# A gated-MLP kernel behind attention: six batches' output projection by seven block products

## The chip, the cores and the metric

The kernel runs on one core of a Trainium2 chip. The metric is the device time of one execution in microseconds. TensorE (PE) does the matmuls and writes their results into eight PSUM banks; VectorE (DVE), ScalarE (ACT) and GpSimd (POOL) work on what lies in the banks or in SBUF (POOL here on SBUF alone); SyncE (SP) issues most of the transfers. Each engine works through its own list in order, and waits where an operand isn't there or a buffer isn't free.

## The reference

Attention with 16 query heads on 4 key and value heads, then a gated MLP with a spatial unit, for 8 batches of 384 tokens. Cut to what matters:

```python
x = attention(q, k, v)                       # (8, 384, 1024)
h = np.maximum(x @ w_in, 0.0)                # w_in (1024, 1024)
u, v = h[..., :512], h[..., 512:]
v_n = (v - mean(v)) / np.sqrt(var(v) + 1e-06)
v_s = np.einsum('ts,bsd->btd', w_spatial, v_n) + b_spatial[None, :, None]
gated = u * v_s                              # (8, 384, 512)
return gated @ w_out                         # w_out (512, 1024)
```

The last line, 384 x 512 by 512 x 1024 for each batch, is what the change is about.

## The kernel before

Tokens come in three tiles of 128 per batch (`NT`), so there are 6 sets of attention work per batch (`SETS`: three tiles by two halves of the heads) and 18 units (`UNITS`). The scores of a set fill six PSUM banks (`units`, L267), ACT takes their exponentials (`exp`, L291), and `weigh` (L295) multiplies them with v, two groups a set, of twelve narrow matmuls each, whose results DVE normalizes by a reciprocal and a product (L315, L317) into `x16`. A transposing transfer (`x_send`, L338) makes `xt` of it.

Everything behind attention is a generator, `gated` (L514), which runs about half a batch behind attention: `pour` (L727) takes matmuls from it in portions of planned time between the parts of a set, so that TensorE's list is a mix of both. For each batch it yields

- `v_part` (L350), three times eight matmuls of 512 columns, into a bank that DVE empties (`vr`, L371); DVE then takes the statistics (`bn_stats`, `bn_aggr`, L383 and L384);
- `u_part` (L433), four blocks of eight matmuls of 384 columns, emptied by ACT (L449). While these run, `root` and `norm` (L386, L393) make the factors on ACT and DVE (`nmr`, L396) and POOL makes `vn` (L401);
- `s_part` (L452), four times three matmuls of 384 columns, to which DVE adds the bias (`vs`, L469) and which POOL multiplies with u into `gT` (L474; DVE does a third of the very last one, L477);
- `o_part` (L482), the output projection: for each of the three token tiles two halves of 512 columns, four matmuls each (L496), copied from the bank into `osb` by DVE, or by ACT for the second half of tile 1 (and others in the last batch), and sent out by SP when both halves are there (L511).

The projection of batch b is made in the generator's batch b + 1: two half tiles behind its first `v_part`, then one ahead of each `s_part` and one behind the last (L517 to L551). In batch 7 one stands behind v and five around s. Batch 7's own projection ends the kernel.

Which bank a group gets is decided when the kernel is written out: `bank` (L79) takes the one that a small model of the engines holds to be free first. `spend` adds planned TensorE time, and `reads` adds the time that an engine is expected to take to empty the bank. Work on DVE that isn't told to the model by a `reads` doesn't exist for it. On the chip TensorE then waits for the real release. `at` (L594) hangs other work, such as casts and loads, on a unit's number.

Of the kernel before, what the change touches and what calls it, by code (L numbers as in the profile page):

```python
# [9 lines left out]
FP32 = mybir.dt.float32  # L10
FP16 = mybir.dt.float16
I32 = mybir.dt.int32
AF = mybir.ActivationFunctionType
ALU = mybir.AluOpType
# [4 lines left out]
def kernel(  # L19
# [14 lines left out]
    nc = tc.nc  # L34
# [52 lines left out]
    def spend(ns):  # L87
        clock[nc.tensor] += ns
# [234 lines left out]
        measure()  # L323

    def new_xt(b):
        xts[b] = att.tile([P, NK, S], FP16, name=f"xt_{b}", tag="xt", bufs=3)

    def x_turn(b, qt, lo, hi, eng):
        if qt == 0 and lo == 0:
# [20 lines left out]
    def v_part(b, st, lo=0, hi=NK):  # L350
        if st == 0 and lo == 0:
            mvs[b] = small.tile([P, NT, 2], FP32, name=f"mv_{b}", tag="mv")
        if lo == 0:
            pvs[b, st] = bank([P, 512], FP32, f"pv_{b}_{st}")
        pv = pvs[b, st]
        for kt in range(lo, hi):
            nc.tensor.matmul(  # L357
                pv,
                xts[b][:, kt, st * P : (st + 1) * P],
                w_in16[:, kt, DH:DFF],  # L360
                start=(kt == 0),
                stop=(kt == NK - 1),
            )
            spend(C512)
            if kt < NK - 1:
                yield C512
        if hi < NK:
            return
        reads(dve, 610.0, f"pv_{b}_{st}")
        vr = moe.tile([P, DH], FP32, name=f"vr_{b}_{st}", tag="vr", bufs=6)  # L370
        dve.tensor_scalar(vr, pv, 0.0, None, op0=ALU.max)  # L371
        v_r[b, st] = vr
        unmeasured.append((b, st))
        if b == B - 1:
            measure()
        yield C512
# [16 lines left out]
    def norm(b):  # L393
        rstd = mvs[b, "rstd"]
        nmr = small.tile([P, NT], FP32, name=f"nmr_{b}", tag="nmr")
        dve.scalar_tensor_tensor(  # L396
            nmr, mvs[b][:, :, 0], -1.0, rstd, op0=ALU.mult, op1=ALU.mult
        )
        for st in range(NT):
            vn = moe.tile([P, DH], FP16, name=f"vn_{b}_{st}", tag="vn", bufs=6)  # L400
            (dve if b == 0 and st == 1 else pool).tensor_scalar(  # L401
                vn,
                v_r.pop((b, st)),
                rstd[:, st : st + 1],
                nmr[:, st : st + 1],
                op0=ALU.mult,
                op1=ALU.add,
            )
            v_n[b, st] = vn
# [6 lines left out]
    def judge():  # L416


        for i, op in enumerate((ALU.max, ALU.min, ALU.add)):
            dve.tensor_reduce(ext[:, i : i + 1], r_all, axis=mybir.AxisListType.X, op=op)  # L420
        pool.memset(ones16, 1.0)
        pool.tensor_scalar(ext[:, 1:2], ext[:, 1:2], 0.0, None, op0=ALU.is_gt)
        pool.tensor_scalar(ext[:, 0:1], ext[:, 0:1], 1.0, ext[:, 1:2], op0=ALU.is_le, op1=ALU.mult)
        pool.tensor_scalar(fine16, ext[:, 2:3], 0.0, ext[:, 0:1], op0=ALU.is_gt, op1=ALU.mult)
# [52 lines left out]
                eng.tensor_tensor(gT[:, :, t], vs[:, :, t], uT[:, :, t], ALU.mult)  # L477
        yield C384

    osbs = {}  # L480

    def o_part(b, tt, half):  # L482
        last = b == B - 1
        if half == 0:
            osbs[b, tt] = ops.tile([P, DM], FP32, name=f"osb_{b}_{tt}", tag="osb")
        osb = osbs[b, tt]
        rows = out[b].rearrange("(p t) d -> p t d", t=NT)

        on_act = half and (last or tt == 1) or last and tt == NT - 1
        parts = [(half * 512, 512, act if on_act else dve, sp)]  # L490
        if last and tt == NT - 1 and half:
            parts = [(512, 256, dve, sp), (768, 128, act, act), (896, 128, dve, sp)]
        for c0, width, eng, queue in parts:
            po = bank([P, 512], FP32, f"po_{b}_{tt}_{c0}")
            for m in range(NM):
                nc.tensor.matmul(  # L496
                    po[:, 0:width],
                    gTs[b][:, m, tt * P : (tt + 1) * P],
                    w_out16[:, m, c0 : c0 + width],
                    start=(m == 0),  # L500
                    stop=(m == NM - 1),
                )
                spend(C512 * width / 512)
                if m < NM - 1:
                    yield C512 * width / 512
            cols = slice(c0, c0 + width)
            copy(eng, osb[:, cols], po[:, 0:width], f"po_{b}_{tt}_{c0}")
            if last or (b, tt) == (B - 2, NT - 1):
                queue.dma_start(rows[:, tt, cols], osb[:, cols])
            elif half:  # L510
                sp.dma_start(rows[:, tt, :], osb)  # L511
            yield C512 * width / 512

    def gated():  # L514
        for b in range(B):
            u0 = b * UNITS
            behind = [(b - 1, tt, half) for tt in range(NT) for half in range(2)] if b else []  # L517
            if b == 0:
                for st in range(NT):
                    yield ("from", 6 * st + 7)  # L520
                    yield from v_part(b, st, 0, 4)
                    yield ("from", 6 * st + 10)
                    yield from v_part(b, st, 4, 8)
            else:
                yield ("from", u0 + 12)
                yield from v_part(b, 0)
                for _ in range(1 if b == B - 1 else 2):
                    yield from o_part(*behind.pop(0))
                yield ("from", u0 + 18)
                yield from v_part(b, 1)  # L530
                yield ("from", u0 + 24)
                yield from v_part(b, 2)
            for m in range(NM):
                i = 0
                for x in u_part(b, m):
                    yield x
                    i += 1
                    if (m, i) == (1, 6):
                        root(b)
                    if (m, i) == (2, 3):  # L540
                        norm(b)
                    if (b, m, i) == (B - 1, 2, 5):
                        judge()
            for m in range(NM):
                if (b, m) == (B - 1, 2):
                    count()
                if behind:
                    yield from o_part(*behind.pop(0))
                yield from s_part(b, m)
            if behind:  # L550
                yield from o_part(*behind.pop(0))  # L551
        for tt in range(NT):
            for half in range(2):
                yield from o_part(B - 1, tt, half)
# [39 lines left out]
    def at(n, f, *args):  # L594
        todo.setdefault(n, []).append((f, args))
# [92 lines left out]
    at(29, load_v, 2)  # L688
    at(31, load_q, 2, 1, sp, (1, 2))
    at(36, cast_v, 2, pool)  # L690
    for j, n in ((0, 34), (1, 36)):
        at(n, cast_q, 2, j, pool, (1, 2))
        at(n + 1, q_send, 2, j, 1, NT)
# [346 lines left out]
```

## Time and profile before

| what | value |
|---|---|
| runs | 237.82, 238.12, 238.57 us; median 238.12 us |
| profiled execution | 238.65 us, of which its span 237.1 us |
| PE, ACT, DVE, POOL busy | 230.4, 170.0, 143.8, 102.2 us |
| 512-column projection matmuls (L496) | 188, 49.6 us busy, 379 ns each with their overlap |
| copies of `osb` by DVE, 512 wide | 37, 686 ns each |
| copies of `osb` by ACT, 512 wide | 10, 592 ns each |
| `x` (L317), 256 wide; `vs` (L469), 384 wide | 424 and 552 ns each |
| `bn_stats`; `vr` | 685 and 682 ns each |
| f16 evictions `qT` (512 wide), `kT` (384 wide) | 422 and 354 ns each |
| `gT` on POOL (L474); `vn` on POOL (L401) | 1058 and 779 ns each |

Matmul records overlap each other, since a matmul starts before the one ahead has left the pipeline; their pace is the distance of two starts, not the duration of one. An idle time in brackets behind a line of the timeline is that of the engine just before the operation, with what ended it.

### The profile page before, as it was taken

The numbers are of one execution on the slowest core, as the hardware profiler recorded it, in microseconds if no ns is written. First come the engines' busy times: TensorE is split into PE (matmuls) and PEld (weight loads), VectorE is DVE, ScalarE is ACT, GpSimd is POOL, SyncE is SP. The second block draws the span as 40 slices with busy tenths as digits, with TensorE's granted clock in tenths as the row PEclk, the third lists the DMA queues.
The fourth block names the chain that finished last, engine by engine and source line by source line (L and its number), as shares of the span: only waits on it lengthen the run. The fifth ranks groups of instructions, "written<-read, shape, count | busy, mean of one in ns | idle before, by whom it ended". The sixth has DMA issues, their size and how long they took to land.

```text
span 237.1 us, 5954 instructions
## 1 busy us (share of the span) xinstructions
PE 230.4 (97%) x2317; PEld 124.3 (52%) x2317; DVE 143.8 (61%) x382; ACT 170.0 (72%) x350; POOL 102.2 (43%) x149
## 2 busy tenths in 40 slices
PE   7899999999999999999999999999999999999993
PEld 6555655545554545555464555554465455545542
DVE  2668774676447674566646576376744667367561
ACT  2899989959897869977797776986697776401212
POOL 3489493642556442275045800575032500460740
PEclk9999999999999999999999999999999999999999
DMA  6999959999999999699988899479912543240266
GB/s 186 289 300 308 275 152 160 169 317 260 296 211 237 258 351 171 214 199 309 188 257 214 241 214 294 68 271 158 255 27 44 114 164 79 48 177 0 86 229 222
DMA packets 67757, 47.48 MB, mean 200 GB/s; under 512 B 48368, under 2 KB 60576, under 8 KB 67728
## 3 DMA queue, kind: packets, MB, share of 16 engines
q1 hardware_dynamic: 62800, 39.86, 68.9%
q0 software_dynamic: 3952, 6.42, 12.3%
q10 hardware_dynamic: 976, 0.82, 1.1%
q8 instruction: 18, 0.29, 0.5%
q14 instruction: 11, 0.09, 0.1%
HBM read 25.95 MB, written 12.58 MB: 163 GB/s over the span
## 4 chain that ended last, share of the span: by engine, by line
PE 91%; DMA 4%; DVE 2%; issue 0%; ACTq 0%; ACT 0%
PE pu L438 18%; PE pv L357 17%; PE po L496 17%; PE sc L281 15%; PE av L301 14%; PE psp L457 7%; DMA q<-in_q_dram 2%; DMA qT<-q 2%; PE qps L240 1%; PE xps L334 1%; DVE x L317 1%; DVE qT L218 0%; DVE osb L218 0%; DVE q L208 0%; ACTq L124 0%
## 5 line engine op out<-in xcount | busy, mean ns | idle before, releaser
L293 ACT ACTIVATE aT<-sc 128x512 f16<-128x512 f32 x288 | 147.5, 617 | 31.4 <-PE sc L281 30.8
L301 PEld LDWEIGHTS <-aT 128*128 128x128 f16 x1152 | 47.0, 97 | 17.3 <-issue 2.3
L357 PE MATMUL pv<-w_in,xt 128*128 128x512 f16 x192 | 51.0, 380 | 0.1
L301 PE MATMUL av<-v,aT 128*128 128x65 f16 x1152 | 50.5, 193 | 0.1
L496 PE MATMUL po<-w_out,gT 128*128 128x512 f16 (+2 forms) x200 | 50.5, 371 | 0.0
L438 PE MATMUL pu<-xt,w_in 128*128 128x384 f16 x256 | 49.9, 327 | 0.0
L401 POOL TENSOR_SCALAR vn<-vr,rstd,nmr 128x512 f16<-128x512 f32 x23 | 17.6, 779 | 67.0 <-DVE nmr L396 45.6
L474 POOL TENSOR_TENSOR gT<-vs,uT 128x384 f16<-128x384 f32 x31 | 32.4, 1058 | 31.8 <-DVE r_all L315 16.9
L317 DVE TENSOR_TENSOR x<-av,r_all 128x256 f16<-128x256 f32 x96 | 40.7, 424 | 3.3
L281 PE MATMUL sc<-qT,kT 64*128 64x512 f16 x288 | 41.5, 380 | 0.3
L315 DVE RECIPROCAL r_all<-av 128x4 f32<-128x4 f32 x96 | 17.1, 178 | 40.6 <-PE av L301 40.3
L218 DVE COPY osb<-po 128x512 f32<-128x512 f32 (+2 forms) x39 | 26.1, 669 | 16.3 <-PE po L496 16.3
L438 PEld LDWEIGHTS <-w_in 128*128 128x128 f16 x256 | 22.1, 98 | 17.1 <-issue 5.5
L449 ACT ACTIVATE uT<-pu 128x384 f16<-128x384 f32 x32 | 15.8, 495 | 16.0 <-PE pu L438 15.8
L496 PEld LDWEIGHTS <-gT 128*128 128x128 f16 x200 | 17.6, 98 | 17.1 <-issue 3.3
L357 PEld LDWEIGHTS <-xt 128*128 128x128 f16 x192 | 15.8, 97 | 17.8 <-issue 5.5
L281 PEld LDWEIGHTS <-kT 64*128 64x128 f16 x288 | 10.9, 94 | 23.5 <-issue 11.9
L457 PE MATMUL psp<-wsT,vn 128*128 128x384 f16 x96 | 22.2, 327 | 0.0
L469 DVE TENSOR_TENSOR vs<-psp,bias_bc 128x384 f32<-128x384 f32 x32 | 17.6, 552 | 7.1 <-PE psp L457 6.9
L371 DVE TENSOR_SCALAR vr<-pv 128x512 f32<-128x512 f32 x24 | 16.4, 682 | 8.4 <-PE pv L357 8.3
L203 POOL CAST q<-q 128x768 f16<-128x768 f32 x22 | 17.6, 830 | 7.9 <-issue 4.3
L383 DVE BATCH_NORM_STATS2 stats<-vr 128x6 f32<-128x512 f32 x24 | 16.4, 685 | 0.1
(55 smaller groups left out, 103.2 us busy)
## 6 DMA issues: line engine op xcount, KB each, us to landing
out_dram<-osb SPq DMA_DIRECT2D x20, 512.0 KB, 3.9
q<-in_q_dram SPq DMA_DIRECT2D x10, 768.0 KB, 5.7
v_None<-in_v_dram SPq DMA_DIRECT2D x6, 384.0 KB, 7.0
w_in<-in_moe_w_in_dram POOLq DMA_DIRECT2D x4, 512.0 KB, 9.8
k_None<-in_k_dram SPq DMA_DIRECT2D x5, 384.0 KB, 3.8
out_dram<-osb SPq DMA_DIRECT2D x7, 256.0 KB, 2.5
q<-in_q_dram POOLq DMA_DIRECT2D x2, 768.0 KB, 7.6
w_out<-in_moe_w_out_dram POOLq DMA_DIRECT2D x2, 512.0 KB, 9.5
```

The costliest lines, as they stand in the source:

```text
L203: eng.tensor_copy(t16[:, :, :, hh, :], src[:, hh])
L218: (act.copy if eng is act else dve.tensor_copy)(o, i)
L281: nc.tensor.matmul(sc, kTs[b][rows, j, kt * P : (kt + 1) * P], qTs[b, j][rows, qt].rearrange("p (r i c) -> p i r c", r=G, i=G), start=True ...
L293: act.activation(a, sc, AF.Exp, scale=scale)
L301: nc.tensor.matmul(av[:, i * (D + 1) : (i + 1) * (D + 1)], aT[:, kt, hh, i * P : (i + 1) * P], v1[b % 2][:, 2 * j + hh, kt, 0 : D + 1], st ...
L317: dve.tensor_tensor(x16s[b][:, qt, c : c + 256].rearrange("p (i d) -> p i d", i=G), o[:, :, 0:D], r.to_broadcast([P, G, D]), ALU.mult,)
L357: nc.tensor.matmul(pv, xts[b][:, kt, st * P : (st + 1) * P], w_in16[:, kt, DH:DFF], start=(kt == 0), stop=(kt == NK - 1),)
L401: (dve if b == 0 and st == 1 else pool).tensor_scalar(vn, v_r.pop((b, st)), rstd[:, st : st + 1], nmr[:, st : st + 1], op0=ALU.mult, op1=A ...
L438: nc.tensor.matmul(pu[:, 0:S], w_in16[:, kt, m * P : (m + 1) * P], xts[b][:, kt, :], start=(kt == 0), stop=(kt == NK - 1),)
L457: nc.tensor.matmul(psp[:, 0:S], v_n[b, st][:, m * P : (m + 1) * P], wsT16[:, st, :], start=(st == 0), stop=(st == NT - 1),)
L474: pool.tensor_tensor(gT, vs, uT, ALU.mult)
L496: nc.tensor.matmul(po[:, 0:width], gTs[b][:, m, tt * P : (tt + 1) * P], w_out16[:, m, c0 : c0 + width], start=(m == 0), stop=(m == NM - 1),)
```

## The change

For batches 1 to 6 (`fast`), the projection of token tiles 0 and 1 is made as one product of a 2 x 2 block matrix (two token tiles by two halves of the 512 gated features) with a 2 x 2 block matrix (two halves of the features by two halves of the 1024 columns). Seven block products replace the eight; each is two matmuls of 512 columns into a bank of its own (`f_part`). Products 5, 6, 7 and 4 take combined weights, products 5, 6, 7 and 3 combined gated values:

- `w_combine` makes the four combinations of the weights, once, in f16 on DVE, at units 42, 45, 48 and 51 (each 1024 elements a partition);
- `g_combine` makes the four combinations of a batch's gated values in f16 on DVE (256 elements a partition each), in the next batch behind its last `v_part`;
- all sums of products are DVE operations that read a bank: product 1 is copied into `partial`, 6 and 7 are added on top of it and of each other, 2 and 1 give tile 0's first half, 5 is read twice, 4 gives the rest of tile 1 and 3 the rest of tile 0. Tile 1 is sent out behind product 4 and tile 0 behind product 3.

The order within the next batch changes too. Tile 2 is made as before, but right behind the first `v_part`; products 1 and 2 stand behind u's block 0, 6 and 7 behind block 1, 5 behind block 2, 4 ahead of the second `s_part` and 3 ahead of the third. In batch 7, tile 2 of batch 6 stands ahead of the fourth `s_part`, and nothing stands behind that; both of its halves are copied by ACT, where DVE copied them before. Batch 0 and batch 7 keep the eight products. Some buffers become fewer: `xt` two instead of three, `vr` four instead of six, `vn` three instead of six.

```diff
@@ -323,7 +323,7 @@
         measure()
 
     def new_xt(b):
-        xts[b] = att.tile([P, NK, S], FP16, name=f"xt_{b}", tag="xt", bufs=3)
+        xts[b] = att.tile([P, NK, S], FP16, name=f"xt_{b}", tag="xt", bufs=2)
 
     def x_turn(b, qt, lo, hi, eng):
         if qt == 0 and lo == 0:
@@ -367,7 +367,7 @@
         if hi < NK:
             return
         reads(dve, 610.0, f"pv_{b}_{st}")
-        vr = moe.tile([P, DH], FP32, name=f"vr_{b}_{st}", tag="vr", bufs=6)
+        vr = moe.tile([P, DH], FP32, name=f"vr_{b}_{st}", tag="vr", bufs=4)
         dve.tensor_scalar(vr, pv, 0.0, None, op0=ALU.max)
         v_r[b, st] = vr
         unmeasured.append((b, st))
@@ -397,7 +397,7 @@
             nmr, mvs[b][:, :, 0], -1.0, rstd, op0=ALU.mult, op1=ALU.mult
         )
         for st in range(NT):
-            vn = moe.tile([P, DH], FP16, name=f"vn_{b}_{st}", tag="vn", bufs=6)
+            vn = moe.tile([P, DH], FP16, name=f"vn_{b}_{st}", tag="vn", bufs=3)
             (dve if b == 0 and st == 1 else pool).tensor_scalar(
                 vn,
                 v_r.pop((b, st)),
@@ -477,7 +477,78 @@
                 eng.tensor_tensor(gT[:, :, t], vs[:, :, t], uT[:, :, t], ALU.mult)
         yield C384
 
-    osbs = {}
+    osbs, halves16, partial = {}, {}, {}
+    w_out_t = cst.tile([P, 4, 2, 512], FP16, name="w_out_t")
+
+    def fast(b):
+
+        return 0 < b < B - 1
+
+    def w_combine(i):
+
+        b11, b12, b21, b22 = (w_out16[:, r : r + 2, c : c + 512] for r in (0, 2) for c in (0, 512))
+        t = [w_out_t[:, k] for k in range(4)]
+        x, y = ((b12, b11), (b22, t[0]), (b22, b12), (t[1], b21))[i]
+        dve.tensor_tensor(t[i], x, y, ALU.subtract)
+
+    def g_combine(b):
+
+        t = halves16[b] = moe.tile([P, 4, 2, P], FP16, name=f"gS_{b}", tag="gS", bufs=1)
+        a11, a12, a21, a22 = (
+            gTs[b][:, r : r + 2, c : c + P] for c in (0, P) for r in (0, 2)
+        )
+        dve.tensor_tensor(t[:, 0], a21, a22, ALU.add)
+        dve.tensor_tensor(t[:, 1], t[:, 0], a11, ALU.subtract)
+        dve.tensor_tensor(t[:, 2], a11, a21, ALU.subtract)
+        dve.tensor_tensor(t[:, 3], a12, t[:, 1], ALU.subtract)
+
+    def f_part(b, n):
+
+        if n == 2:
+            for tt in range(2):
+                osbs[b, tt] = ops.tile([P, DM], FP32, name=f"osb_{b}_{tt}", tag="osb")
+        if n == 1:
+            partial[b] = moe.tile([P, 3, 512], FP32, name=f"part_{b}", tag="part", bufs=1)
+        g, s, w, t = gTs[b], halves16.get(b), w_out16, w_out_t
+        left, right = {
+            1: (lambda m: g[:, m, 0:P], lambda m: w[:, m, 0:512]),
+            2: (lambda m: g[:, 2 + m, 0:P], lambda m: w[:, 2 + m, 0:512]),
+            3: (lambda m: s[:, 3, m], lambda m: w[:, 2 + m, 512:1024]),
+            4: (lambda m: g[:, 2 + m, P : 2 * P], lambda m: t[:, 3, m]),
+            5: (lambda m: s[:, 0, m], lambda m: t[:, 0, m]),
+            6: (lambda m: s[:, 1, m], lambda m: t[:, 1, m]),
+            7: (lambda m: s[:, 2, m], lambda m: t[:, 2, m]),
+        }[n]
+        name = f"pf_{b}_{n}"
+        po = bank([P, 512], FP32, name)
+        for m in range(2):
+            nc.tensor.matmul(po, left(m), right(m), start=(m == 0), stop=(m == 1))
+            spend(C512)
+            if m == 0:
+                yield C512
+        s1, s2, s3 = (partial[b][:, k] for k in range(3))
+        s4 = s1
+        lo, hi = slice(0, 512), slice(512, 1024)
+        if n == 1:
+            copy(dve, s1, po, name)
+        else:
+            o, x, y, op = {
+                2: (osbs[b, 0][:, lo], po, s1, ALU.add),
+                6: (s2, po, s1, ALU.add),
+                7: (s3, po, s2, ALU.add),
+                5: (s4, po, s2, ALU.add),
+                4: (osbs[b, 1][:, lo], s3, po, ALU.subtract),
+                3: (osbs[b, 0][:, hi], po, s4, ALU.add),
+            }[n]
+            if n == 5:
+                reads(dve, 690.0)
+                dve.tensor_tensor(osbs[b, 1][:, hi], po, s3, ALU.add)
+            reads(dve, 690.0, name)
+            dve.tensor_tensor(o, x, y, op)
+        for tt, end in ((0, 3), (1, 4)):
+            if n == end:
+                sp.dma_start(out[b].rearrange("(p t) d -> p t d", t=NT)[:, tt, :], osbs[b, tt])
+        yield C512
 
     def o_part(b, tt, half):
         last = b == B - 1
@@ -486,7 +557,7 @@
         osb = osbs[b, tt]
         rows = out[b].rearrange("(p t) d -> p t d", t=NT)
 
-        on_act = half and (last or tt == 1) or last and tt == NT - 1
+        on_act = half and (last or tt == 1) or b >= B - 2 and tt == NT - 1
         parts = [(half * 512, 512, act if on_act else dve, sp)]
         if last and tt == NT - 1 and half:
             parts = [(512, 256, dve, sp), (768, 128, act, act), (896, 128, dve, sp)]
@@ -514,7 +585,24 @@
     def gated():
         for b in range(B):
             u0 = b * UNITS
-            behind = [(b - 1, tt, half) for tt in range(NT) for half in range(2)] if b else []
+            plain = [(b - 1, tt, half) for tt in range(NT) for half in range(2)]
+            order = {}
+            if not b:
+                pass
+            elif fast(b - 1):
+                at_u, at_s = ((1, 2), (6, 7), (5,), ()), ((), (4,), (3,), ())
+                for m in range(NM):
+                    order["u", m], order["s", m] = at_u[m], at_s[m]
+                order["v" if b < B - 1 else ("s", NM - 1)] = plain[4:]
+            elif b < B - 1:
+                order = {"v": plain[:2], **{("s", m): plain[2 + m : 3 + m] for m in range(NM)}}
+            else:
+                order = {"v": plain[:1], **{("s", m): plain[1 + m : 2 + m] for m in range(NM + 1)}}
+
+            def behind(place):
+                for x in order.get(place, ()):
+                    yield from f_part(b - 1, x) if isinstance(x, int) else o_part(*x)
+
             if b == 0:
                 for st in range(NT):
                     yield ("from", 6 * st + 7)
@@ -524,12 +612,13 @@
             else:
                 yield ("from", u0 + 12)
                 yield from v_part(b, 0)
-                for _ in range(1 if b == B - 1 else 2):
-                    yield from o_part(*behind.pop(0))
+                yield from behind("v")
                 yield ("from", u0 + 18)
                 yield from v_part(b, 1)
                 yield ("from", u0 + 24)
                 yield from v_part(b, 2)
+                if fast(b - 1):
+                    g_combine(b - 1)
             for m in range(NM):
                 i = 0
                 for x in u_part(b, m):
@@ -541,14 +630,13 @@
                         norm(b)
                     if (b, m, i) == (B - 1, 2, 5):
                         judge()
+                yield from behind(("u", m))
             for m in range(NM):
                 if (b, m) == (B - 1, 2):
                     count()
-                if behind:
-                    yield from o_part(*behind.pop(0))
+                yield from behind(("s", m))
                 yield from s_part(b, m)
-            if behind:
-                yield from o_part(*behind.pop(0))
+            yield from behind(("s", NM))
         for tt in range(NT):
             for half in range(2):
                 yield from o_part(B - 1, tt, half)
@@ -688,6 +776,8 @@
     at(29, load_v, 2)
     at(31, load_q, 2, 1, sp, (1, 2))
     at(36, cast_v, 2, pool)
+    for i in range(4):
+        at(42 + 3 * i, w_combine, i)
     for j, n in ((0, 34), (1, 36)):
         at(n, cast_q, 2, j, pool, (1, 2))
         at(n + 1, q_send, 2, j, 1, NT)
```

## The prediction

> **What bounds the kernel now.** I read the page first: busy shares, the slices, the chain.
>
> ```profile
> PE 230.4 (97%) x2317; PEld 124.3 (52%) x2317; DVE 143.8 (61%) x382; ACT 170.0 (72%) x350; POOL 102.2 (43%) x149
> PE   7899999999999999999999999999999999999993
> PEclk9999999999999999999999999999999999999999
> PE 91%; DMA 4%; DVE 2%; issue 0%; ACTq 0%; ACT 0%
> ```
>
> TensorE is full from the second slice to the last, at full clock, and 91% of the chain that ended last is matmuls. So the time moves by what a change takes from the list of matmuls, less what it makes them wait. Then the timeline, for the pace of a projection matmul:
>
> ```profile
> 129.68 0.38 PE L496 MATMUL po<-w_out,gT 128*128 128x512 f16 x1
> 151.79 1.03 PE L496 MATMUL po<-w_out,gT 128*128 128x512 f16 x4
> ```
>
> Three more matmuls cost 1.03 - 0.38 = 0.65 us: 0.216 each. In the same way a 384-column matmul costs 0.1625, a group of twelve 65-column ones 0.36, and a set of six scores 0.85 with the changes around it.
>
> Third, the timeline of DVE where batch 6 goes from v to u, the place that matters most below:
>
> ```profile
> 195.18 0.18 DVE L315 RECIPROCAL r_all<-av 128x4 f32<-128x4 f32 x1 [1.18 <-PE av L301]
> 195.40 0.42 DVE L317 TENSOR_TENSOR x<-av,r_all 128x256 f16<-128x256 f32 x1
> 195.74 0.68 DVE L371 TENSOR_SCALAR vr<-pv 128x512 f32<-128x512 f32 x1
> 196.63 0.18 DVE L315 RECIPROCAL r_all<-av 128x4 f32<-128x4 f32 x1 [0.21 <-PE av L301]
> 196.84 0.42 DVE L317 TENSOR_TENSOR x<-av,r_all 128x256 f16<-128x256 f32 x1
> 197.18 0.68 DVE L383 BATCH_NORM_STATS2 stats<-vr 128x6 f32<-128x512 f32 x1
> 197.90 0.18 DVE L384 BATCH_NORM_AGGREGATE mv<-stats 128x2 f32<-128x6 f32 x1
> 198.00 0.66 DVE L371 TENSOR_SCALAR vr<-pv 128x512 f32<-128x512 f32 x1
> 199.58 0.18 DVE L315 RECIPROCAL r_all<-av 128x4 f32<-128x4 f32 x1 [0.92 <-PE av L301]
> ```
>
> It shows DVE's pace (an operation that doesn't need its predecessor starts some 0.08 us before that one's end, so r_all and x together cost 0.55, stats and mv 0.82, vr 0.60), and that DVE has only short rests here. Last, what happens where it is late:
>
> ```profile
> 80.91 0.67 DVE L218 COPY osb<-po 128x512 f32<-128x512 f32 x1
> 81.63 0.52 PE L301 MATMUL av<-v,aT 128*128 128x65 f16 x12
> 81.63 0.40 PEld L301 LDWEIGHTS <-aT 128*128 128x128 f16 x11 [0.28 <-issue]
> ```
>
> The copy ends at 81.58, and av, which has the copied bank next, starts at 81.63, 0.16 us later than its predecessor's pace allows. A bank that DVE frees late stops TensorE within 0.05 us. After 82 us the old kernel loses no more than 0.14 us in any such place.
>
> **The change, part by part.**
>
> *Seven products for eight.* Fourteen matmuls of 512 columns instead of sixteen, per batch, in six batches: 12 x 0.216 = **-2.59 us**. Their weights load under the neighbours as now (98 ns against 216).
>
> *DVE's new work.* A batch's two tiles cost DVE three copies of 0.69 us before and ACT a fourth; now DVE has eight PSUM operations (tile 2's two copies stay with it, but for batch 6, where ACT gets both). The sums (512 wide, from PSUM and SBUF) have no row; x (256 wide, 0.424) and vs (384 wide, 0.552) rise by 1.0 ns per element, so 0.68. The gated sums (256 wide, all f16 in SBUF) have none either. The f16 evictions qT and kT (512 wide 0.42, 384 wide 0.35) rise by 0.52 ns per element, which gives 0.29; the ends are r_all's 0.18, almost nothing but the fixed cost, and x's 0.42. I take 0.29, since all operands are 16 bits wide as in qT: the four cost 1.06 at DVE's pace. By rows DVE's batch rises from about 17.6 to 22 us of some 28, so the question is where it is late.
>
> *Waits for banks.* I laid DVE's new order, with these paces, against the new order of matmuls and the bank that each group gets. The planner counts no time for the gated or the weight sums, so it hands out banks too early. The worst place, products of batch 5 inside batch 6: from the recip of the last av before it, DVE has r_all and x 0.55, stats and mv 0.82, vr 0.60, the four gated sums 1.06, r_all and x 0.55, stats and mv 0.82, product 1's copy 0.69: free at 5.09. TensorE has from 0.20 us earlier: two pv (0.43), u's block 0 (1.30), an av (0.36), products 1 and 2 (0.86), a score set (0.85), so 3.81: at 3.61 it wants to start u's block 1 in product 1's bank. Wait 5.09 + 0.06 - 3.61 = 1.54 us. In the same way for batches 1 to 4: 0.14, 0.16, 0.18, 0.75. Between s and the next v, where products 4 and 3 sit between the vs sums: 0.13, 0.13, 0.07, 0.25 (batch 5 has free banks there, because attention has ended). Together 3.35. The same laying out of the old kernel gives up to 0.13 where its trace lost nothing, so I take 0.1 off each of nine: **+2.4 us**. With gated sums of 0.18 it is 1.5, with 0.42 it is 4.2. The stall gives DVE time to catch up, so nothing later inherits it.
>
> The Trainium skill (Perfetto Trace Analysis, "Optimizing Scalar/DVE Operations") puts DVE's fixed cost at about 125 ns for a PSUM operand and says that the profiled time holds an acknowledgement that overlaps the next instruction. The overlap is seen here as the 0.08 us; but 512 elements at the 1.0 ns above plus 125 ns is 0.64, an estimate from that page, against the 0.60 measured, which would lengthen the worst wait by some 0.2 us. The measured pace is used.
>
> *Weight sums* (1024 wide f16, once, units 42 to 51). At 0.52 ns per element 0.69 each, by vs's slope 1.2. One is ahead of the r_all that frees a bank for scores: 0.24 late by the same laying out, less 0.1: **+0.15**; at 1.2 two such places and 1.1 us, at best nothing.
>
> *The end.* Attention is over by 203 us, and TensorE runs the remaining blocks alone. Before, a half tile of batch 6 (0.86 us) stood behind the last s block:
>
> ```profile
> 226.88 2.32 PE L496 MATMUL po<-w_out,gT 128*128 128x512 f16 x10
> 227.20 0.55 DVE L469 TENSOR_TENSOR vs<-psp,bias_bc 128x384 f32<-128x384 f32 x1
> 227.85 0.45 DVE L477 TENSOR_TENSOR gT<-vs,uT 128x128 f16<-128x128 f32 x1
> 228.35 0.57 PEld L496 LDWEIGHTS <-gT 128*128 128x128 f16 x4 [0.30 <-DVE gT L477]
> ```
>
> The weights wait for gT until 228.35, 1.47 us after the last s matmul's pace ended at 226.88; matmuls can use them 0.1 later, just when the seven ahead (1.51) are through. The new order puts both halves of tile 2 ahead of that s block, so only three matmuls (0.65) cover it: 1.47 + 0.1 - 0.65, **+0.9 us**. Also, the half tile between u and s of batches 6 and 7 is gone, and nmr stands behind the adds of products 6 and 7:
>
> ```profile
> 218.75 0.16 DVE L396 SCALAR_TENSOR_TENSOR nmr<-mv,rstd 128x3 f32<-128x3 f32 x1 [0.67 <-ACT rstd L390]
> 219.12 2.27 POOL L401 TENSOR_SCALAR vn<-vr,rstd,nmr 128x512 f16<-128x512 f32 x3 [6.85 <-PE pu L438]
> ```
>
> nmr to the last vn takes 2.64, and s needs that vn at its third matmul. In batch 7, from product 7's end: 0.20 to DVE, 0.3 left of product 6's add, its own 0.69, nmr to vn 2.64, the load 0.1, less one overlap of 0.08: 3.85; TensorE has u 1.30, product 5 0.43, u 1.30, two s matmuls 0.33, 3.36: +0.45. In batch 6, with an attention group in between but r_all and x on DVE too, +0.4 beyond the 0.14 that it loses now. End: **+1.75**, from 1.2 to 2.0.
>
> *At nothing:* fewer buffers (xt, vr, vn): each is last read at least half a batch (about 14 us) before its next writer. On SP's queue the same number of output transfers now come in pairs behind products 4 and 3; the x transposes behind them are issued two score sets (8 us) before v reads them, against the sum's delay of about 1 us. Without that cover each would cost that 1 us a batch. ACT loses a copy (0.59) per batch and isn't late; POOL's list is unchanged.
>
> *Sum:* -2.59 + 2.4 + 0.15 + 1.75 = **+1.7 us** on the span of 237.1, so 238.8. That profiled execution took 238.65 in all, 1.55 outside the span, and 0.53 above the median of the runs. On the median: 238.12 + 1.7, **239.8 us**.
>
> **The rivals.**
> - *Faster: DVE is in time.* If the banks come free where the planner thinks, as old TensorE's lack of loss after 82 us suggests, then -2.59 and only the end's covers remain; with half of those hidden, -1.7: 236.4. Against it: between v and u DVE rests 0.92 us in the old trace and gets 2.3 us more (gated sums, product 1, product 2). It decides from where the worst wait is under 0.3 us.
> - *A draw:* small bank waits (1.5) and no weight-sum wait, an end of 1.2: +0.1, 238.2.
> - *DVE becomes the bound:* the gated and weight sums run at the slow ends (0.42 and 1.2): -2.59 + 4.2 + 1.1 + 1.75 = +4.5, 242.6. For it: f32 rows only rise at 1 ns per element, and no row has two f16 inputs.
> - *The change doesn't do what it says:* if a product's two short groups didn't overlap their neighbours, the 12 matmuls wouldn't be saved: +4.3, 242.4. Against it: one-matmul pieces of po already run at pace between score sets.
>
> **How the numbers follow.** Forecast 0.53, heavy DVE 0.17, not saved 0.03, a draw 0.14, faster 0.13. The measurement tells 0.3%, 0.7 us, from no change, so the forecast's small end adds a little to the draw: slower 0.69, same 0.17, faster 0.14. The terms' ends give -2.59 + 1.5 + 0 + 1.2 = +0.1 and -2.59 + 4.2 + 1.1 + 2.0 = +4.7; leaving out the corner of all bad ends and reaching down halfway to the faster case: 237.2 to 242.2. The forecast's own range is 238.8 to 241.2.
>
> **What would show it.** PE's matmul count down by 12 records, at 0.216. Gated sums of about 0.29 us and weight sums of 0.69. A TensorE gap of 1 to 1.6 us before u's block 1 in batch 6 and of 0.5 to 0.8 in batch 5, released by DVE's copy of product 1; 0.9 us before the last tiles behind gT; 0.4 before s in batches 6 and 7 behind vn. I am wrong if those gaps are missing, if TensorE's gaps sum to under 2 us (then faster), or if the time is lost in front of score sets behind ACT or a transfer, which I cost at nothing.

## The result and the profile after

The changed kernel takes 241.15 us (median of 4 runs, 240.88 to 242.59) where the old one takes 238.34 beside it: a ratio of 1.0122, with a 95% interval of 1.0084 to 1.016, so slower by 1.2%. The profiled execution has a span of 239.7 us against 237.1. Medians and ratios here and below leave out the one slow run of all, 241.13 us of the kernel in which only the order is changed. First the page of the new kernel: busy shares, two rows of the 40 slices, the chain.

```profile
PE 230.3 (96%) x2305; PEld 123.0 (51%) x2305; DVE 168.6 (70%) x438; ACT 168.0 (70%) x346; POOL 102.6 (43%) x149
...
PE   7999999999999999999999999999999998899993
...
PEclk9999999999999999999999999999999999999999
...
PE 11%; POOL 1%; issue 1%; DVE 1%; DVEq 0%; POOLq 0%
```

Twelve matmul records fewer, 2317 to 2305, as forecast, at full clock, and yet PE's busy time is the same 230 us: the ends of matmuls are modelled, and part of the waiting counts as busy. The row of slices shows the loss only as two 8s near the end. The chain, 91% matmuls before, now explains 14% of the span and breaks off. None of the three says where 2.6 us went.

What does is the distance between the starts of two matmuls less the pace of the first (0.216 us for 512 columns, 0.163 for 384, 0.756 for a whole set of six scores, 0.096 more for a step into scores; my own sum from the trace, gaps of 0.02 us and up, past 60 us, where both kernels have left the first loads behind):

| lost past 60 us | before | after |
|---|---|---|
| scores at the second weight sum (62.96) | 0 | 0.72 |
| batch 1's products (92.5, 101 to 103) | 0.12 | 0.77 |
| batch 2's, batch 3's products | 0 | 0.11, 0.21 |
| batch 4's products (171.8 to 186) | 0 | 0.77 |
| batch 5's products (199.6, 201.9) | 0 | 1.37 |
| batch 6: s waits for vn (208.8, 209.6) | 0.14 | 1.02 |
| batch 7: s waits for vn (225.4: 0.51), the small matmul `count` behind it for POOL (226.6: 0.08) | 0 | 0.59 |
| the end: last tiles wait for gT (231.1) | 0 | 0.72 |
| the same in both (69.8, 76.1, 81.7) | 0.28 | 0.28 |
| sum | 0.54 | 6.56 |

So 6.02 lost and 2.59 saved: +3.43. The trace agrees with that sum: the set of scores at 62.96 starts 0.68 earlier than its like before (63.64; the first loads came sooner in this execution), and the last matmul 2.75 later (235.64 against 232.88): 3.43 between them.

The worst place, batch 6 between v and u, in the timeline (start, duration, engine, line, operation, count, and in brackets the idle time before it with its releaser):

```profile
196.96 0.18 DVE L315 RECIPROCAL r_all<-av 128x4 f32<-128x4 f32 x1 [1.71 <-PE av L301]
...
198.34 0.68 DVE L371 TENSOR_SCALAR vr<-pv 128x512 f32<-128x512 f32 x1
...
198.93 0.28 DVE L500 TENSOR_TENSOR gS<-gT 128x256 f16<-128x256 f16 x1
...
199.25 0.29 DVE L501 TENSOR_TENSOR gS<-gS,gT 128x256 f16<-128x256 f16 x1
...
200.07 0.42 DVE L317 TENSOR_TENSOR x<-av,r_all 128x256 f16<-128x256 f32 x1
200.41 0.69 DVE L383 BATCH_NORM_STATS2 stats<-vr 128x6 f32<-128x512 f32 x1
200.55 0.09 PEld L281 LDWEIGHTS <-kT 64*128 64x128 f16 x1 [0.62 <-DVE x L317]
...
201.23 0.66 DVE L218 COPY part<-pf 128x512 f32<-128x512 f32 x1
...
201.94 0.48 PE L438 MATMUL pu<-xt,w_in 128*128 128x384 f16 x2 [0.68 <-DVE part L218]
```

DVE runs without a rest from r_all at 196.96 to the copy's end at 201.89. TensorE is held twice on the way: the last pair of scores waits for the bank that x frees (at 200.55, 0.51 lost), then u's block 1 for the bank of product 1 (0.86 lost), 0.05 behind the copy.

Batch 6 between u and s, the same view:

```profile
206.88 0.15 DVE L396 SCALAR_TENSOR_TENSOR nmr<-mv,rstd 128x3 f32<-128x3 f32 x1
...
207.24 2.27 POOL L401 TENSOR_SCALAR vn<-vr,rstd,nmr 128x512 f16<-128x512 f32 x3 [18.47 <-PE pf L525]
...
208.82 0.34 PE L457 MATMUL psp<-wsT,vn 128*128 128x384 f16 x1 [0.27 <-POOL vn L401]
...
209.57 0.34 PE L457 MATMUL psp<-wsT,vn 128*128 128x384 f16 x1 [0.41 <-POOL vn L401]
```

rstd is ready at 202.0, but nmr comes at 206.88, behind the adds of products 6 and 7 and a pair of r_all and x; POOL's three vn end at 209.51, and s waits for the second and the third. Before, nmr stood at 203.30, right behind that pair's x:

```profile
203.30 0.15 DVE L396 SCALAR_TENSOR_TENSOR nmr<-mv,rstd 128x3 f32<-128x3 f32 x1
```

At the end of the changed kernel:

```profile
229.96 0.56 DVE L469 TENSOR_TENSOR vs<-psp,bias_bc 128x384 f32<-128x384 f32 x1 [1.47 <-PE psp L457]
...
230.63 0.45 DVE L477 TENSOR_TENSOR gT<-vs,uT 128x128 f16<-128x128 f32 x1
...
231.13 1.69 PE L567 MATMUL po<-w_out,gT 128*128 128x512 f16 x7 [0.56 <-DVE gT L477]
```

Three matmuls at 229.76 are all the cover there is, and 0.72 us is open.

### The profile page after: what moved, and what is told of

Read it like the earlier page. It is cut to its first block, busy times and chain, and to the rows that moved or that the text cites. A ratio compares the mean times of both kernels' runs of the same rounds, so it can differ in the third digit from the quotient of the medians.

```text
span 239.7 us, 5973 instructions
## 1 busy us (share of the span) xinstructions
PE 230.3 (96%) x2305; PEld 123.0 (51%) x2305; DVE 168.6 (70%) x438; ACT 168.0 (70%) x346; POOL 102.6 (43%) x149
## 5 line engine op out<-in xcount | busy, mean ns | idle before, releaser
L401 POOL TENSOR_SCALAR vn<-vr,rstd,nmr 128x512 f16<-128x512 f32 x23 | 18.1, 798 | 83.1 <-DVE nmr L396 32.8
L438 PE MATMUL pu<-xt,w_in 128*128 128x384 f16 x256 | 51.8, 326 | 0.7 <-DVE part L218 0.7
L281 PE MATMUL sc<-qT,kT 64*128 64x512 f16 x288 | 43.2, 380 | 1.2 <-DVE x L317 0.3
L474 POOL TENSOR_TENSOR gT<-vs,uT 128x384 f16<-128x384 f32 x31 | 31.7, 1071 | 17.6 <-DVE vs L469 11.2
L567 PE MATMUL po<-w_out,gT 128*128 128x512 f16 (+2 forms) x104 | 25.2, 363 | 0.6 <-DVE gT L477 0.6
L457 PE MATMUL psp<-wsT,vn 128*128 128x384 f16 x96 | 21.5, 326 | 1.0 <-POOL vn L401 1.0
L218 DVE COPY osb<-po 128x512 f32<-128x512 f32 (+2 forms) x19 | 12.3, 647 | 8.3 <-PE po L567 8.2
L567 PEld LDWEIGHTS <-gT 128*128 128x128 f16 x104 | 8.8, 97 | 11.4 <-issue 3.6
```

The lines of the kernel that those rows point to most:

```text
L281: nc.tensor.matmul(sc, kTs[b][rows, j, kt * P : (kt + 1) * P], qTs[b, j][rows, qt].rearrange("p (r i c) -> p i r c", r=G, i=G), start=True ...
L401: (dve if b == 0 and st == 1 else pool).tensor_scalar(vn, v_r.pop((b, st)), rstd[:, st : st + 1], nmr[:, st : st + 1], op0=ALU.mult, op1=A ...
L438: nc.tensor.matmul(pu[:, 0:S], w_in16[:, kt, m * P : (m + 1) * P], xts[b][:, kt, :], start=(kt == 0), stop=(kt == NK - 1),)
L457: nc.tensor.matmul(psp[:, 0:S], v_n[b, st][:, m * P : (m + 1) * P], wsT16[:, st, :], start=(st == 0), stop=(st == NT - 1),)
L474: pool.tensor_tensor(gT, vs, uT, ALU.mult)
L567: nc.tensor.matmul(po[:, 0:width], gTs[b][:, m, tt * P : (tt + 1) * P], w_out16[:, m, c0 : c0 + width], start=(m == 0), stop=(m == NM - 1),)
```

## The experiments

All were timed against the old kernel on the same chip; ratios have their 95% interval. In each, "lost" is the sum of the table above.

**Is the planner's blindness the cause?** (DVE's sums told to the bank model.)

```diff
     def w_combine(i):
+        reads(dve, 750.0)
     def g_combine(b):
+        reads(dve, 1060.0)
```

> The planner that hands out banks is told of DVE's time for the gated sums (1060 ns) and each weight sum (750 ns). Theory: the gated sums stand ahead of the copies on DVE, so that every bank comes free late, whichever is chosen; laying out DVE's order against the new banks leaves the waits ahead of u's block 1 in batches 5 and 6 where they are (0.4 and 1.1 us in the changed kernel's trace) and takes away only those behind the weight sums (0.7 us in sets 2.4 and 3.0). Span 239 to 239.7 against 239.7. Rival: the planner's blindness is the cause, and with the truth it finds free banks: the waits ahead of block 1 vanish, 1.5 to 2 us less, about 237.8.

Measured: 241.26 us, ratio 1.0109 [1.0081, 1.0137]; lost 6.04. The weight sum's wait went from 0.72 to 0.31, batch 4's two (at scores and at u) from 0.66 to 0.56, and batch 5's stayed at 1.36. Told of the gated sums, the planner finds no bank there that comes free sooner: its blindness is a cause at the weight sums alone. Even of those 0.41 us only half belongs to that, since weight sum 2 itself was 0.20 us shorter here than the 1.17 of the changed kernel (why it varies is shown below):

```profile
62.32 0.97 DVE L493 TENSOR_TENSOR w_out_t<-w_out,w_out_t 128x1024 f16<-128x1024 f16 x1
```

**Is it the time of the gated sums on DVE?** Moved to POOL in one run, doubled in another:

```diff
-        dve.tensor_tensor(t[:, 0], a21, a22, ALU.add)
+        pool.tensor_tensor(t[:, 0], a21, a22, ALU.add)
...
```

> The four gated sums of a batch are made by POOL, everything else as in the changed kernel. Theory: DVE's queue loses 1.06 us just where it is late. The wait ahead of u's block 1 in batch 6 falls from 1.14 to 0.1-0.4 us, that in batch 5 from 0.43 to under 0.1, batch 2's by 0.4: 1.2 to 1.8 us less in all, span 237.9 to 238.5. Rival: the eight PSUM sums alone fill DVE, the gated ones only happen to stand there: less than 0.4 us, span 239.3 or more; or POOL's slower sums delay vn and the time moves there.

> The four gated sums are made twice in a row, nothing else changes. Theory: DVE has no rest between v and u, so the 1.06 us more per batch become TensorE waits almost in full in batches 2, 3, 5 and 6 and in part in batch 4: by the laying out +0.6, +1.0, +0.3, +1.0, +1.0 and up to 0.5 through nmr in batch 7: 3.5 to 4.4 us more, span 243 to 244. Rival: DVE (70% busy) has room, and the time was lost elsewhere: +0.5 or less.

Measured with POOL: 239.94, 1.0059 [1.0038, 1.008], lost 4.45. The timeline at batch 5's place:

```profile
198.44 0.69 DVE L383 BATCH_NORM_STATS2 stats<-vr 128x6 f32<-128x512 f32 x1
...
199.26 0.66 DVE L218 COPY part<-pf 128x512 f32<-128x512 f32 x1
...
199.97 0.48 PE L438 MATMUL pu<-xt,w_in 128*128 128x384 f16 x2 [0.26 <-DVE part L218]
```

The wait for the score bank is gone and that for product 1's bank is 0.43; 0.94 of 1.37 went with four sums that hold DVE for 0.93 us (from 198.93 to the r_all behind them at 199.86). Batch 4's went from 0.77 to 0.34, batch 1's from 0.77 to 0.48. The waits for vn and gT stayed (0.99, 0.56, 0.79). The lost sum fell by 2.11, more than the 1.2 to 1.8 expected, but 0.51 of that is at the weight sum, which the edit doesn't touch.

Doubled: 245.95, 1.0318 [1.0275, 1.0361], lost 9.97, span 243.4 as expected. At batch 5's place:

```profile
203.33 0.39 PE L281 MATMUL sc<-qT,kT 64*128 64x512 f16 x1 [1.06 <-DVE x L317]
...
204.71 0.48 PE L438 MATMUL pu<-xt,w_in 128*128 128x384 f16 x2 [0.68 <-DVE part L218]
```

The four sums more hold DVE for another 0.93 us (201.70 to 202.63 in that trace), and TensorE loses another 0.93 us at the score bank (1.44 lost) and nothing more at u's block 1: once DVE sets the pace, its whole queue is passed on, to the first matmul that wants a bank.

**The order of the end**, one part alone (the halves of tile 2 in batch 7 set apart, so that one covers the last gT), then the whole order of batches 6 and 7:

```diff
-                order["v" if b < B - 1 else ("s", NM - 1)] = plain[4:]
+                if b < B - 1:
+                    order["v"] = plain[4:]
+                else:
+                    order["s", 0], order["s", NM] = plain[4:5], plain[5:]
```

> In batch 7 alone the two halves of batch 6's tile 2 are put where a half tile stood in the kernel before: one ahead of the first s block and one behind the last. Theory: the 0.51 us that s waits for vn and the 0.72 us that the last tiles wait for gT in the changed kernel's trace fall to under 0.1 us each, span 1.1 to 1.3 us lower, 238.5. The second wait for vn, in batch 6 (0.43 and 0.59 us), stays. Rival: these waits hide others (banks, the copies on ACT, the last transfers), and the gain is under 0.4 us.

Measured: 240.92, 1.0099 [1.0069, 1.013], lost 5.23. The waits of batch 7's s are gone (0.59), that for gT only fell from 0.72 to 0.49: 0.82 by the edit, where 1.1 to 1.3 were expected. (The lost sum fell by another 0.51 at weight sum 2, which this edit doesn't touch. The set of scores there starts 0.5 us later than in the changed kernel's trace, so that the span, 239.1, shows less of all this.) At the end something else was late:

```profile
226.78 3.24 POOL L474 TENSOR_TENSOR gT<-vs,uT 128x384 f16<-128x384 f32 x3 [0.25 <-DVE vs L469]
...
229.39 0.79 DVE L477 TENSOR_TENSOR gT<-vs,uT 128x128 f16<-128x128 f32 x1
...
230.07 1.69 PE L567 MATMUL po<-w_out,gT 128*128 128x512 f16 x7 [0.33 <-POOL gT L474]
```

POOL makes three gT in a row without a rest and ends at 230.02; the last tiles now wait for POOL's gT of block 2.

The whole order, all else as in the change:

```diff
+                if b >= B - 2:
+                    at_u = ((), (1, 2), (6, 7), (5,))
-                order["v" if b < B - 1 else ("s", NM - 1)] = plain[4:]
+                if b < B - 1:
+                    order["v"] = plain[4:]
+                else:
+                    order["s", NM - 1], order["s", NM] = plain[4:5], plain[5:]
```

> Only the order in the generator's batches 6 and 7 is that of the repaired kernel (products 1 and 2 behind u's block 1, 6 and 7 behind block 2, 5 behind block 3, tile 2's halves around the last s block). DVE makes the gated sums, the planner knows nothing of them. Theory: of the changed kernel's waits the 1.14 us in batch 6's u (its last part), the 1.02 and 0.59 us of s behind vn and the 0.72 us behind gT go, those of batches 1 to 4 stay: span 236.3 to 236.8 against 239.7. The rest up to the repaired kernel (about 1.3 us) is what the gated sums on DVE and the weight sums cost in batches 1 to 5. Rival: nmr is late for another reason than the adds of products 6 and 7 (ACT, statistics), and s waits as before: 238 or more.

Measured: 238.25, 1.0000 [0.9976, 1.0025], lost 3.12. Moving each product of batches 5 and 6 one block of u later takes away batch 5's two waits and all vn waits:

```profile
204.36 2.28 POOL L401 TENSOR_SCALAR vn<-vr,rstd,nmr 128x512 f16<-128x512 f32 x3 [15.53 <-DVE nmr L396]
...
206.92 0.65 PE L457 MATMUL psp<-wsT,vn 128*128 128x384 f16 x3
```

The span is 236.5, as expected. vn starts 2.9 us earlier, 1.4 of it by the missing waits at u, the rest because nmr has products 6 and 7 behind it. The wait for gT, expected to go too, only fell from 0.72 to 0.42: the last tiles now wait for POOL's gT of block 2, as in the run before. This order alone brings the time back to the old kernel's.

**All three together** (the best kernel, below): POOL's gated sums, the weight sums told to the planner, and this order.

> Three repairs in one. POOL makes the gated sums; the planner counts 750 ns for each weight sum; in the generator's batches 6 and 7 products 1 and 2 stand behind u's block 1, 6 and 7 behind block 2, 5 behind block 3, and in batch 7 the halves of tile 2 stand ahead of and behind the last s block. Theory: all that stands against the 2.59 us of saved matmuls is these waits. Left are the small ones of batches 1 to 5 (0.5 us together): span 234.8 to 235.5, 0.7 to 1.0% faster than before. Rival: TensorE's gaps only move, or the twelve matmuls weren't worth 2.6 us; then not under 236.5.

Measured: 237.35, 0.9952 [0.9927, 0.9977], span 235.6 for the 234.8 to 235.5 expected: 0.5% faster than the old kernel, and so faster than both. Lost 1.89, of which 0.41 at gT and the rest in pieces of 0.03 to 0.27.

```profile
PE 228.2 (97%) x2305; PEld 122.9 (52%) x2305; DVE 163.2 (69%) x414; ACT 168.1 (71%) x346; POOL 117.4 (50%) x173
...
L438 PE MATMUL pu<-xt,w_in 128*128 128x384 f16 x256 | 51.7, 326 | 0.0
...
L457 PE MATMUL psp<-wsT,vn 128*128 128x384 f16 x96 | 21.0, 326 | 0.0
```

The groups (busy time, mean ns | idle before) show no idle time ahead of u and s, where the change had 0.7 and 1.0; by the distances of starts 0.31 us is still lost there in three small places.

**Are twelve matmuls worth 2.59?** The old kernel without two of the four matmuls of tile 0's first half in batches 1 to 6 (its output holds half of that sum there):

```diff
-            for m in range(NM):
+            for m in range(2 if 0 < b < B - 1 and (tt, half) == (0, 0) else 0, NM):
```

> The kernel before, with two of the four matmuls left out of the first half of tile 0's projection in batches 1 to 6, so these columns hold half of their sum: twelve matmuls fewer and no other change. Theory: TensorE is the bound, and they are worth 12 x 0.216: span 234.4 to 234.7, median ratio 0.989. Rival: part of the saved time falls into waits for ACT or transfers: 235.5 or more.

Measured: 236.92, 0.9936 [0.9916, 0.9956], lost 1.55. It saves 1.6, not 2.6: three gaps of 0.38 us ahead of v, behind DVE's copies of `osb`, one of 0.18 behind POOL's gT and one of 0.09 take the place of 0.42 lost before, and give 1.0 back. So a pure cut is passed on in part only, too, and the four larger gaps stand behind DVE and POOL, not behind the ACT or the transfers of the rival. The first of the three:

```profile
80.89 0.38 PE L357 MATMUL pv<-w_in,xt 128*128 128x512 f16 x1 [0.22 <-DVE osb L218]
```

**Do the smaller buffers cost anything?** The old kernel with xt 2, vr 4 and vn 3. (The new kernel with the old numbers has no run.)

```diff
-        xts[b] = att.tile([P, NK, S], FP16, name=f"xt_{b}", tag="xt", bufs=3)
+        xts[b] = att.tile([P, NK, S], FP16, name=f"xt_{b}", tag="xt", bufs=2)
...
```

> The kernel before with the changed kernel's fewer buffers (xt 2, vr 4, vn 3) and nothing else. Theory: each buffer is read for the last time half a batch before its next writer, so nothing waits: span within 0.4 us of 237.1. Rival: transfers into xt or DVE's vr wait for TensorE or POOL, and a part of the changed kernel's loss is this: 237.8 or more.

Measured: 238.96, 1.0017 [0.9999, 1.0035], lost 1.28, with a span of 237.5, just within the 0.4 expected. DVE and POOL stand idle ahead of vr and vn for as long as before (8.6 and 66.0 us in all, against 8.4 and 67.0), so nothing is seen to wait for these buffers. Two losses are new. One is 0.21 ahead of the scores at 72.13, which wait for a qT that lands at 72.00: SP came to its transfer late, because it was held for 3.50 us at an xt transfer before it (1.55 in the old kernel, 2.45 in the changed one, which doesn't have this loss):

```profile
58.09 3.50 SPq L341 DMA_TRANSPOSE xt<-x  x1
```

Whether the smaller xt has a part in that is not shown. The other is 0.53 at the end, on engines that use none of the three buffers there:

```profile
228.04 0.76 POOL L477 TENSOR_TENSOR gT<-vs,uT 128x256 f16<-128x256 f32 x1 [0.34 <-DVE vs L469]
...
228.36 0.65 DVE L477 TENSOR_TENSOR gT<-vs,uT 128x128 f16<-128x128 f32 x1 [0.46 <-DVE vs L469]
```

DVE's third took 0.65 us beside POOL's, against 0.45 before, which is 0.20 of the 0.53. The remainder is the idle time of DVE ahead of it, 0.46 us against 0.10 before; what held DVE there the trace doesn't show. The longer third led to the last experiment.

**Does POOL slow DVE's gT?** The best kernel with all three thirds of the last gT on DVE:

```diff
-            for eng, t in ((dve, slice(0, 1)), (pool, slice(1, NT))):
+            for eng, t in ((dve, slice(i, i + 1)) for i in range(NT)):
```

> e5_best with one more edit: all three thirds of the very last gT are made on DVE, so POOL works on nothing once its earlier gT have ended (226.64 us in e5_best). If DVE's third is slow because POOL works on the same kind of operation at the same time, the third that runs beside POOL's earlier gT takes 0.65 to 0.79 us again, and the two behind it, with POOL idle, clearly less: by r_all's 0.18 us and the 1 ns per element of the PSUM rows some 0.3 us each, at most 0.45. If instead the duration belongs to the operation and its strides, all three take the same. The time would be within 0.3 us of e5_best, 237.1 to 237.6 us, since the end waits for the first third and for POOL's gT of the block before alike.

Measured: 237.34, 0.9937 [0.9911, 0.9964], no different from the best kernel. The tile's view (duration min/median/max):

```profile
L477 DVE TENSOR_TENSOR gT<-vs,uT x3: 481/486/792, 227.2 to 228.0; 128x128 f16<-128x128 f32 x3
```

The first, beside POOL's gT, took 0.79; the two others are recorded with 0.48, but start 0.2 us before their predecessor's end, and the three ends (227.96, 228.25, 228.53) lie 0.29 and 0.28 apart, the 0.3 expected. So the first is longer because of POOL, and this explains more than the end. The second weight sum of the changed kernel, in its timeline:

```profile
61.15 1.60 POOL L203 CAST q<-q 128x768 f16<-128x768 f32 x2 [2.75 <-DMA q<-in_q_dram]
...
62.13 1.17 DVE L492 TENSOR_TENSOR w_out_t<-w_out,w_out_t 128x1024 f16<-128x1024 f16 x1
...
63.90 0.60 PE L281 MATMUL sc<-qT,kT 64*128 64x512 f16 x3 [0.34 <-DVE x L317]
```

and in the run with POOL's gated sums, where the cast had ended at 62.28:

```profile
62.30 0.66 DVE L492 TENSOR_TENSOR w_out_t<-w_out,w_out_t 128x1024 f16<-128x1024 f16 x1
```

DVE operations with both inputs in SBUF that start beside one of POOL's, in us of each trace:

| run, operation | starts | POOL's operation ends | ends | after POOL |
|---|---|---|---|---|
| changed kernel, weight sum 2 | 62.13 | 62.75 | 63.29 | 0.54 |
| changed kernel, weight sum 3 | 66.06 | 66.48 | 67.02 | 0.54 |
| order of batches 6, 7, weight sum 2 | 62.34 | 62.81 | 63.35 | 0.54 |
| best kernel, weight sum 1 | 57.81 | 58.08 | 58.62 | 0.54 |
| tile 2 apart in batch 7, last gT's third | 229.39 | 230.02 | 230.18 | 0.16 |
| best kernel, last gT's third | 226.01 | 226.63 | 226.80 | 0.17 |
| fewer buffers, last gT's third | 228.36 | 228.80 | 229.01 | 0.21 |

Alone, a weight sum takes 0.66 to 0.68. Of the 19 in all runs that start beside a POOL operation, 18 end 0.53 to 0.57 behind that one's end, whatever the overlap: DVE stands until POOL is through. In the other (sums doubled, weight sum 3) POOL's vn is recorded as starting only 0.05 us ahead; there the sum took 0.68 and it was vn that took 1.29. The Trainium skill (SBUF — State Buffer, "SBUF: two separate sides") states this as an exclusive lock on a port pair that the two engines share, which a DVE operation with two SBUF inputs takes against a GpSimd operation that reads SBUF, and by which the later one blocks for the whole instruction. These rows agree on DVE's side; sums with one input in PSUM (part, osb) keep to 0.68 or 0.69 throughout. And the wait of the scores follows the sum's duration: where the planner isn't told, 0.21, 0.30, 0.56 and 0.72 lost for sums of 0.66, 0.75, 1.01 and 1.17, one for one.

All runs in one table; the middle column takes off before's 0.54 and the 2.59 of the matmuls (for the buffers, which save none, the 0.54 alone):

| kernel | lost | less 0.54 and 2.59 | median against before's |
|---|---|---|---|
| the change | 6.56 | +3.43 | +2.81 |
| planner told | 6.04 | +2.91 | +2.65 |
| gated sums on POOL | 4.45 | +1.32 | +1.33 |
| tile 2 apart in batch 7 | 5.23 | +2.10 | +2.31 |
| gated sums doubled | 9.97 | +6.84 | +7.34 |
| order of batches 6, 7 | 3.12 | -0.01 | -0.28 |
| together | 1.89 | -1.24 | -1.18 |
| together, last gT on DVE | 2.27 | -0.86 | -1.29 |
| matmuls left out | 1.55 | -1.58 | -1.61 |
| fewer buffers | 1.28 | +0.74 | +0.43 |

The sum of one profiled execution accounts for the median of many to within 0.1 us in three of the ten and to 0.62 at most. It leaves out how a single execution begins: the set of scores that starts at 63.64 in the old kernel's trace starts between 62.90 and 64.21 in the others.

## Why the prediction was right, and where it was short

The forecast, 239.8, was on the right side and 1.35 us low (+1.7 on the old median, against +2.8). Its sign was no luck: none of its four terms had the wrong sign, and the three losses were each, as a whole, taken too low, so that no error of one covered for another's. But some 1.1 us of the loss, in batch 1 and at the weight sums, came by ways that were not in the working. By its steps, measured past 60 us:

- *Seven products for eight, -2.59:* the records are down by 12 at 0.216, so it holds. That such a cut needn't arrive whole (1.6 of 2.59 in the run without the matmuls) I hadn't considered.
- *Prices of the new work:* the gated sums take 0.275 to 0.292 us by line (0.29 taken), but the four hold DVE for 0.93 us and not 1.06; the sums from PSUM 0.68 to 0.69, a weight sum alone 0.66 to 0.68 (0.69 taken). All three had been read off rows of other operations by their slopes. The groups of the changed kernel:

```profile
L547 DVE TENSOR_TENSOR part<-pf,part 128x512 f32<-128x512 f32 x18 | 12.3, 685 | 1.6 <-PE pf L525 1.0
...
L501 DVE TENSOR_TENSOR gS<-gS,gT 128x256 f16<-128x256 f16 x6 | 1.8, 292 | 0.2
L502 DVE TENSOR_TENSOR gS<-gT 128x256 f16<-128x256 f16 x6 | 1.7, 284 | 0.0
```

- *Waits for banks, +2.4:* 3.11. Batches 4 and 5 came out as laid out (0.77 for 0.80, 1.37 for 1.44, the 0.1 taken off), though both are split between the score bank (0.51 in each) and u (0.15 and 0.86), and the first was not named. In batch 5 DVE took 4.93 from r_all to the copy's end (5.09 laid out, most of the difference in the gated sums) and TensorE 3.81 of its own, as laid out. Batch 1 failed: 0.65 net for 0.07. There DVE stands 0.41 us ahead of product 2's add between two of its semaphore instructions, with nothing to wait for that I could find: the releaser that the profile names, qT's transfer, ended at 92.90 in the run with POOL's sums, where the same add began at 92.12. The pause is 0.41 in four programs (the change, the planner told, and the two that alter only the end) and missing where the gated sums ahead of it are on POOL or doubled, so it seems to go with the place in DVE's instruction list; what it is stays open.
- *Weight sums, +0.15:* 0.72. The mis-sized step. Alone they would have cost 0.21 (0.24 laid out); the other 0.51 is DVE standing behind POOL's cast. That two engines exclude each other on such operands was not in the working at all.
- *The end, +1.75:* 2.19. gT 0.72 for 0.9, batch 7's vn 0.59 with the count behind it for 0.45 (its own terms give 0.49), batch 6's vn 0.88 more than before for 0.4. The last was waved through instead of summed. Summed from the trace, from product 7's end at pace (204.83): DVE has 0.11 to the add of product 6, which x of the group before had held up until 204.94, the two adds 1.39, r_all and x 0.55, nmr to the last vn 2.63 and 0.06 to TensorE, 4.74; TensorE has 3.72 up to the third s matmul; 1.02.
- *At nothing:* in the changed kernel every loss of 0.4 us and more stands behind DVE or POOL, and none behind a smaller buffer, a transfer or ACT, as said. In the old kernel with the smaller buffers the 0.21 us behind a late qT stays open.

Of the rivals, "DVE becomes the bound" was half right, in its place though not in its price: wherever its queue is full, TensorE waits for all of it, 0.93 us lost for 0.93 more of sums. "DVE is in time" fell with the 1.37 at batch 5, which was to decide it at 0.3. That the planner's blindness makes the waits, on which the forecast rested ("so it hands out banks too early"), is refuted for the gated sums: told of them, it finds no better bank. The waits came from DVE's list alone, which the forecast had laid out.

## What to carry over

When an operation saved on the full engine is paid with work on another, lay that engine's list out by its recorded paces between two fixed points and see how late each buffer comes free; it gave 1.44 for a measured 1.37. Here it helped little to tell the planner, and much to move the new work behind the operations that others wait for: the same products of the last two batches one block later, with 0.93 us a batch of sums on the engine that had most time to spare, turned +2.8 us into -1.2 (with the weight sums told to the planner, too). Where a DVE operation with two SBUF inputs can meet a POOL operation, as the weight sums met casts, vn and gT, the two engines are laid out as one queue.

## What the hardware showed beyond this

- DVE and POOL exclude each other on such operands in both directions: POOL's vn beside weight sum 3 took 1.20 us (0.76 to 0.77 otherwise) and a gT beside weight sum 4 took 1.43 (1.05 to 1.08). Two SBUF tensors on DVE aren't the only case: batch 0's vn on POOL, at 38.69, took 1.02 beside DVE's own vn, which reads one. In the changed kernel's timeline:

```profile
70.67 0.68 DVE L492 TENSOR_TENSOR w_out_t<-w_out_t,w_out 128x1024 f16<-128x1024 f16 x1
```

```profile
70.84 1.43 POOL L474 TENSOR_TENSOR gT<-vs,uT 128x384 f16<-128x384 f32 x1 [2.41 <-DVE vs L469]
```

- A gated sum on POOL took 0.67 us where DVE takes 0.28, in the tile's view of the run with the sums on POOL:

```profile
L500 POOL TENSOR_TENSOR gS<-gT x6: 668/669/672, 85.0 to 212.9; 128x256 f16<-128x256 f16 x6
```

- Scores start in pairs (distances of 0.004, 0.22, 0.004, 0.21, 0.004, 0.31 us in an undisturbed set), so a held pair costs its whole delay, although the profile puts less of it down as idle: 0.34 us at 63.90 for 0.72 lost, and at 200.55 so little that the view shows none for PE (0.13), for 0.51.
